# A windowed attention and MLP kernel: blocks of 48 queries instead of 56, values cast into window-ready rows, and a new opening order

## The chip, the cores and the metric

The kernel runs on one core of a Trainium2 chip. The metric is the device time of one execution in microseconds. A profiled execution gives the trace; its span runs from the first to the last instruction. Engines are named as the profile names them: PE (TensorE, with PEld for its weight loads), DVE (VectorE), ACT (ScalarE), POOL (GpSimd), SP (SyncE, which issues transfers). POOL's transfers run on the DMA queue q0, SP's on q1.

## The reference

Attention over 576 positions with a window of 32 to either side and 8 global positions (which attend to all and are attended by all), for 8 batches and 8 heads of 64; its output, seen as 4608 rows of 512, goes through an MLP whose activation is h cos h.

```python
def _attn_ref(q, k, v, global_idx):            # q, k, v: 8 x 8 x 576 x 64, fp32
    scores = np.matmul(q, k.transpose(0, 1, 3, 2)) / np.sqrt(D)
    mask = np.abs(pos[:, None] - pos[None, :]) <= 32
    mask = mask | is_global[:, None] | is_global[None, :]
    scores = np.where(mask, scores, -1e9)
    attn = np.exp(scores - np.max(scores, axis=-1, keepdims=True))
    attn = attn / (np.sum(attn, axis=-1, keepdims=True) + 1e-09)
    return np.matmul(attn, v)

def reference(...):
    x = attn_out.transpose(0, 2, 1, 3).reshape(4608, 512)
    h = x @ w_in                                # 512 x 2048
    return (h * np.cos(h)) @ w_out              # 2048 x 512
```

## The kernel before

**Tiling of attention.** Work goes by pairs of heads, 32 in all: pair `pr` is batch `pr // 4`, heads `2 (pr % 4)` and the next. A batch's 576 queries are cut into NB = 11 blocks of QB = 56 (the last block is partly padding). A block's keys are the 8 global ones and a window of W = 120, 128 in all, which fill the partitions; its queries are the 8 global ones and its own 56, C = 64 columns a head, two heads beside each other. `scores` multiplies, for four blocks at a time, keys (`kw`, the weights) by queries (`qb`), takes exp on ACT (`e`) and multiplies by `mask` on DVE (`pm`). `values` multiplies each block's `pm` (weights, 64 columns) by the block's window of values `vw` (64 values and a one, which gives the denominator) into `pv`, and normalizes into `xn`. `turn_x` transposes `xn` on PE into `xT`; for every fourth pair POOL copies the eight global queries' columns into `xT` (L483).

**Where keys, queries and values come from.** A half `s` is 4 heads, two pairs; there are 16. For the first four halves `load_qk` has POOL load keys and queries with a cast to fp16 into `kn`, `qn`, and `turned`, called by `local_k` and `local_q`, transposes them on PE; ACT and DVE copy them into `kw` and `qb`. For later halves `cast_half` has POOL write fp16 copies `k16`, `q16` to DRAM, `turn_half` has SP load them transposed into `kT`, `qT`, and DVE copies the blocks out. Values of every half are cast to `v16` in DRAM as they lie; `load_v` then has SP gather each pair's overlapping windows from it, one row of 64 values (128 bytes) per key, block and head; `load_vg` does the same for the global values. `vw`, `kw` and `qb` have four buffers. `gather` fetches the rows of the global positions; `build_globals` casts and transposes them, for 16 pairs at once. `globals_k` and `globals_q` (POOL) copy them into `kw` and `qb`.

**The MLP.** `mlp_in(t, f)` makes one of 16 groups of hidden units for 512 rows: four matmuls, a cosine on ACT, a product on DVE. `mlp_out(t, u)` adds four of 16 hidden groups to an output tile. They fill PE between the parts of attention.

**Order.** The order on each engine is the program's order, written by hand. It begins with set-up code; then the list `FRONT` names the first steps (`s2.0` is scores of pair 2, part 0; `k`, `q` local keys and queries; `g` globals; `p` values; `x` turn_x; `L` load_qk; `c` the cast of a half's values; `v` load_v and load_vg; `W` a quarter of w_in; `n` x_squares; `I` register loads). Then a loop runs steps s = 2 to 15, two pairs each, by the list `THIRD` for s = 2 and `ORDER` after that: `1` is a call of `mlp_in`, `2` one of `mlp_out`, letters `a`, `z`, `c`, `d` stand for pairs 2s to 2s + 3, and `G` calls `casts(s)`, where POOL waits for `xn` of the step (the gate, L662) and issues the casts of a later half (half 4 in step 2, half 5 in step 3, two halves in step 4, then one a step). `w_out` is loaded in one transfer at the beginning of step 2. At each step's end SP issues `turn_half(s + 2)` and the loads of values for pairs 2s + 4 and 2s + 5. After the loop the MLP work that is left runs alone.

Of the kernel before, what the change touches and what calls it, by code (L numbers as in the profile page):

```python
# [21 lines left out]
QB = 56  # L22
NB = 11
G = 8
W = 120
BP = 6
KL = 32
HY = 4
RW = 8
KPAD = 4  # L30
KP = KPAD + S // RW + 10
QP = S // RW + 6
KT = KL + S + 80
QT = S + 48
# [6 lines left out]
ORDER = "sa0 sa1 sa2 2 2 2 sz0 2 sz1 sz2 pa 1 1 2 xa pz G 1 1 2 xz n 1 1 2 kc qc 1 kd qd 2 1"  # L41

THIRD = "sa0 sa1 sa2 sz0 sz1 sz2 1 1 pa 1 1 xa pz G 1 1 kc qc xz 1 1 kd qd 1 n 1"

FRONT = ("s0.0 s0.1 s0.2 s1.0 s1.1 s1.2 k2 q2 g4 L2 p0 k3 q3 s2.0 s2.1 s2.2 g5 W0 c2 p1 x0 g6 W1 s3.0 s3.1 s3.2 g7 I "
         "p2 x1 L3 v4 v5 p3 x2 k4 q4 x3 W2 k5 q5 n0 W3 c3 v6 v7")
# [145 lines left out]
def kernel(  # L192
# [22 lines left out]
    ident16 = const.tile([P, P], FP16)  # L215
    pio2 = const.tile([P, 1], FP32)
# [7 lines left out]
    nc.sync.dma_start(gidx_col, dview(gi, 0, (0, 16), (2, G), (1, 1)))  # L224
    nc.sync.dma_start(gidx_all, dview(gi, 0, (0, P), (1, 2 * G)))
    nc.sync.dma_start(gidx_row, dview(gi, 0, (2 * G, 1), (1, 2 * G)))
# [4 lines left out]
    v16 = dram.tile([B * H * S, D], FP16)  # L231
# [4 lines left out]
    qT = [keep.tile([P, 2, QT], FP16, name=f"qT{i}") for i in range(2)]  # L236
    kn = [keep.tile([KP, 2 * 2, RW, D], FP16, name=f"kn{i}") for i in range(2)]
    qn = [keep.tile([QP, 2 * 2, RW, D], FP16, name=f"qn{i}") for i in range(2)]
    vw = [keep.tile([P, NB, 2, D + 1], FP16, name=f"vw{i}") for i in range(NV)]
    NK = 4  # L240
    kw = [keep.tile([P, NB, P], FP16, name=f"kw{i}") for i in range(NK)]
    qb = [keep.tile([P, NB, 2, C], FP16, name=f"qb{i}") for i in range(NK)]

    def cast_half(s, which):

        base = s * 4 * S * D
        for x in which:
            if x == "v":
                nc.gpsimd.dma_start(v16[s * 4 * S : (s + 1) * 4 * S].rearrange("(n r) d -> n (r d)", r=16),
                                    dview(v, base, (16 * D, 4 * S // 16), (1, 16 * D)))  # L250
            else:
                src, dst = {"k": (k, k16), "q": (q, q16)}[x]
                nc.gpsimd.dma_start(dst[s].rearrange("t (h d) -> t h d", h=4),  # L253
                                    dview(src, base, (D, S), (S * D, 4), (1, D)))

    def load_qk(s):

        base = s * 4 * S * D
        for src, dst in ((k, kn[s % 2][KPAD : KPAD + S // RW]), (q, qn[s % 2][0 : S // RW])):
            nc.gpsimd.dma_start(dst.rearrange("x h r d -> x h (r d)"),  # L260
                                dview(src, base, (RW * D, S // RW), (S * D, 4), (1, RW * D)))

    def turn_half(s):

        nc.sync.dma_start(kT[s % 2][:, :, KL : KL + S], k16[s], transpose=True)
        nc.sync.dma_start(qT[s % 2][:, :, 0:S], q16[s], transpose=True)


    qg32 = keep.tile([P, 2, 2, D], FP32)
    kg32 = keep.tile([P, 2, 2, D], FP32)  # L270
    vg32 = keep.tile([P, 2, 2, D], FP32)
# [6 lines left out]
    def index_rows():  # L278
# [5 lines left out]
        nc.vector.scalar_tensor_tensor(gidx_rows, p8, float(2 * S // G), gidx_col, ALU.mult, ALU.add)  # L284

    def gather(src, dst, half):
        rows = src.rearrange("b h s d -> (b h s) d")
        for h in range(2):
            nc.gpsimd.indirect_dma_start(
                out=dst[:, half, h], out_offset=None, in_=rows,  # L290
                in_offset=bass.IndirectOffsetOnAxis(ap=gidx_rows[:, 0:1], axis=0),
                element_offset=(half * 32 + h) * S * D)

    vg16 = keep.tile([P, 2, 2, D], FP16)

    def load_v(pr):


        b, h0 = pr // NP, 2 * (pr % NP)
        vt = vw[pr % NV]  # L300
        for h in range(2):
            lo, i0, i1 = (b * H + h0 + h) * S * D, 0, NB
            if pr == 0 and h == 0:
                nc.sync.dma_start(vt[G + 32 : P, 0, h, 0:D], dview(v16, 0, (D, W - 32), (1, D)))
                i0 = 1
            if pr % 2 and h:

                nc.sync.dma_start(vt[G : G + 104, NB - 2, h, 0:D], dview(v16, lo + 472 * D, (D, 104), (1, D)))  # L308
                nc.sync.dma_start(vt[G : G + 48, NB - 1, h, 0:D], dview(v16, lo + 528 * D, (D, 48), (1, D)))
                i1 = NB - 2  # L310
            nc.sync.dma_start(vt[G:P, i0:i1, h, 0:D],
                              dview(v16, lo + (QB * i0 - 32) * D, (D, W), (QB * D, i1 - i0), (1, D)))

    def load_vg(pr):
        for h in range(2):
            nc.sync.dma_start(
                vw[pr % NV][0:G, :, h, 0:D],
                view(vg16[(pr % 16) * G : (pr % 16 + 1) * G, pr // 16, h], (0, NB), (1, D)))


    mask = keep.tile([P, NB, 2, C], FP16)

    def build_mask():
# [24 lines left out]
        nc.vector.tensor_scalar(own, df[:, 0:1], float(W), None, ALU.is_lt)  # L348
        nc.vector.memset(own[0:G], 0.0)
        for h in range(2):  # L350
            nc.vector.tensor_tensor(
                mask[:, :, h, G:], view(nk, (1, NB), (0, QB)), view(band[:, G:], (0, NB), (1, QB)), ALU.mult)
            nc.vector.tensor_scalar(
                mask[:, :, h, 0:G], view(val, (1, NB), (0, G)), own[:, 0:1], None, ALU.mult)
# [18 lines left out]
    def build_globals(half):  # L373
        for src, dst in ((kg32, kgT), (qg32, qgT)):
            g16 = work.tile([P, P], FP16, tag="g16")
            nc.scalar.copy(g16, src[:, half].rearrange("x h d -> x (h d)"))
            t = ps.tile([P, 16 * G], FP16, tag="s", bufs=3)
            nc.tensor.transpose(t, g16, ident16)
            nc.scalar.copy(dst[:, 16 * half : 16 * half + 16], t.rearrange("x (n g) -> x n g", g=G))
        nc.scalar.copy(vg16[:, half], vg32[:, half])  # L380
# [4 lines left out]
    xT = keep.tile([P, NC, NT + 40], FP16)  # L385
# [15 lines left out]
    def turned(src, pr, n):  # L401

        t = ps.tile([P, RW, n], FP16, tag="h" if front[0] else "s", bufs=2 if front[0] else 3)
        h0 = 2 * (pr % 2)
        for r in range(RW):
            for h in range(2):
                nc.tensor.transpose(t[h * D : (h + 1) * D, r], src[:n, h0 + h, r], ident16[:n, :n])  # L407
        return t

    def local_k(pr):  # L410
        to = kw[pr % NK][:, :, G:]
        if pr < 2 * HY:
            t = turned(kn[pr // 2 % 2], pr, KP)
            nc.scalar.copy(view(to, (P, NB), (RW, W // RW), (1, RW)),  # L414
                           view(t, (QB // RW, NB), (1, W // RW), (KP, RW)))
        else:
            nc.vector.tensor_copy(to, view(kT[pr // 2 % 2][:, pr % 2], (QB, NB), (1, W)))

    def local_q(pr):
        if pr < 2 * HY:  # L420
            t = turned(qn[pr // 2 % 2], pr, QP)
        for h in range(2):
            hp = slice(h * D, (h + 1) * D)
            to = qb[pr % NK][hp, :, h, G:]
            if pr < 2 * HY:
                copy = nc.scalar.copy if h == 0 or pr < 2 else nc.vector.tensor_copy
                copy(view(to, (2 * C, NB), (RW, QB // RW), (1, RW)),
                     view(t[hp], (QB // RW, NB), (1, QB // RW), (QP, RW)))
# [3 lines left out]
    def scores(pr, g):  # L432
        kp, qp = kw[pr % NK], qb[pr % NK]
        if g == 0:
            pm_of[pr] = work.tile([P, NB, 2, C], FP16, tag="pm", name="pm")
        pm = pm_of[pr]
        g0, n = 4 * g, min(4, NB - 4 * g)
        st = ps.tile([P, 4, P], FP32, tag="s", bufs=3)
# [322 lines left out]
```

## Time and profile before

| | |
|---|---|
| runs | 396.44, 393.04, 397.9 us; median 396.44 |
| the profiled execution | 397.13 us; span 395.4 us; granted TensorE clock 0.955 |
| PE busy | 328.3 us (83%), 2678 matmuls |
| PEld busy | 174.7 us (44%) |
| DVE busy | 260.6 us (66%) |
| ACT busy | 238.8 us (60%) |
| POOL busy | 114.8 us (29%) |
| DMA packets | 188504, 47.18 MB; 177005 of them under 512 bytes |
| q1 (SP's transfers) | 124509 packets, 27.89 MB, 59.6% of 16 engines' span |
| q0 (POOL's transfers) | 63952 packets, 18.75 MB, 48.4% |

Busy shares are means over stages with different limits, and matmuls are pipelined, so a busy PE is one that has work in it. A queue's share is the time of its packets as a part of 16 engines' time; with several packets under way at once the shares can add up to more than 100%. "Us" in a row's second column is the length of a piece, and a line such as L311 is the line of the kernel that issued the instruction.

### The profile page before, as it was taken

How to read it: one execution, taken by the hardware profiler on the slowest of the kernel's cores; microseconds unless marked ns; L12 is line 12 of the kernel's file. 1: busy time of each engine (PE TensorE's matmuls, PEld its weight loads, DVE VectorE, ACT ScalarE, POOL GpSimd, SP SyncE). 2: the span in 40 equal slices, each digit the busy share in tenths (PEclk: the TensorE clock that was granted, in tenths of full speed). 3: DMA queues.
4: the chain of work that ended last, by engine and by line, in shares of the span. 5: the costliest groups of instructions: out<-in, count | busy, mean ns of one | idle time of the engine just before them, and what ended most of it. 6: DMA issues, size and time to landing. Idle time of an engine off the chain costs nothing.

```text
span 395.4 us, 7373 instructions
## 1 busy us (share of the span) xinstructions
PE 328.3 (83%) x2678; PEld 174.7 (44%) x2678; DVE 260.6 (66%) x600; ACT 238.8 (60%) x351; POOL 114.8 (29%) x250
## 2 busy tenths in 40 slices
PE   0272179576778889899999999999999979999993
PEld 0262164343434355455555555555555334444441
DVE  7744157555687768789788888888889354544300
ACT  1572066945575686677778678776777866244210
POOL 6573032504268275071443507223000100000000
PEclk9997558969999999999999999999999999999999
DMA  6989979999999999999999999999990000010121
GB/s 92 96 123 199 123 43 181 215 130 124 176 121 177 108 175 131 166 154 180 149 176 187 127 177 140 191 141 120 144 118 31 27 2 27 28 54 27 55 80 60
DMA packets 188504, 47.18 MB, mean 119 GB/s; under 512 B 177005, under 2 KB 183405, under 8 KB 188205
## 3 DMA queue, kind: packets, MB, share of 16 engines
q1 hardware_dynamic: 124509, 27.89, 59.6%
q0 software_dynamic: 63952, 18.75, 48.4%
q8 instruction: 23, 0.38, 0.5%
q14 instruction: 20, 0.16, 0.2%
HBM read 47.73 MB, written 21.23 MB: 174 GB/s over the span
## 4 chain that ended last, share of the span: by engine, by line
PE 67%; DMA 10%; DVE 8%; ACT 5%; issue 3%; SPq 3%; another core or an unknown queue 1%; POOL 0%; ACTq 0%; DVEq 0%
PE po L505 28%; PE ph L491 27%; DMA q<-in_q_dram 4%; PE st L440 4%; PE pv L452 4%; DMA vw<-vg 3%; DMA vw<-v 3%; DVE g L495 2%; PE tx L475 2%; SPq L308 2%; ACT cos L494 2%; DVE xn L463 1%; PE t L407 1%; ACT sq L524 1%
## 5 line engine op out<-in xcount | busy, mean ns | idle before, releaser
L491 PE MATMUL ph<-xT,w_in 128*128 128x512 f16 x576 | 142.8, 385 | 6.7 <-DVE g L495 5.9
L505 PE MATMUL po<-w_out,g 128*128 128x512 f16 x576 | 140.4, 380 | 5.0 <-DMA w_out<-in_moe_w_out_dram 3.6
L494 ACT ACTIVATE cos<-ph,pio 128x512 f16<-128x512 f32 x144 | 97.3, 686 | 77.2 <-PE ph L491 75.6
L495 DVE TENSOR_TENSOR g<-cos,ph 128x512 f16<-128x512 f16 x144 | 96.4, 685 | 55.0 <-ACT cos L494 52.7
L505 PEld LDWEIGHTS <-g 128*128 128x128 f16 x576 | 55.4, 98 | 67.7 <-issue 5.2
L491 PEld LDWEIGHTS <-w_in 128*128 128x128 f16 x576 | 54.1, 99 | 69.4 <-issue 13.1
L442 ACT ACTIVATE e<-st 128x512 f16<-128x512 f32 (+1 forms) x96 | 47.6, 561 | 14.3 <-PE st L440 9.3
L443 DVE TENSOR_TENSOR pm<-e,mask 128x512 f16<-128x512 f16 (+1 forms) x96 | 37.0, 405 | 23.8 <-ACT e L442 21.9
L662 POOL COPY gate<-xn 1x1 f16<-1x1 f16 x14 | 2.5, 182 | 143.3 <-DVE xn L463 143.3
L452 PE MATMUL pv<-vw,pm 128*64 128x65 f16 x704 | 20.6, 204 | 23.1 <-issue 10.3
L440 PE MATMUL st<-qb,kw 128*128 128x128 f16 x352 | 30.8, 238 | 4.2 <-ACT e L442 1.5
L440 PEld LDWEIGHTS <-kw 128*128 128x128 f16 x352 | 26.3, 108 | 14.2 <-POOL xT L483 2.9
L463 DVE TENSOR_TENSOR xn<-pv,r_all 128x768 f16<-128x768 f32 x32 | 30.6, 958 | 1.9
L452 PEld LDWEIGHTS <-pm 128*64 128x64 f16 x704 | 16.6, 117 | 27.3 <-issue 19.0
L253 POOL DMA_DIRECT2D q<-in_q_dram x12 | 27.6, 2304 | 0.0
L414 ACT COPY kw<-t 128x1320 f16<-128x1320 f16 x8 | 10.1, 1257 | 28.7 <-PE t L407 28.7
L483 POOL COPY xT<-xg 128x4 f16 x64 | 20.5, 320 | 22.0 <-DVE xT L478 18.6
L510 ACT COPY o<-po 128x512 f32<-128x512 f32 x18 | 10.5, 586 | 22.4 <-PE po L505 21.9
L524 ACT ACTIVATE sq<-xn 128x1536 f16<-128x1536 f16 x16 | 23.6, 1474 | 0.0
L430 DVE COPY qb<-qT 64x616 f16<-64x616 f16 x48 | 22.1, 460 | 0.3
L253 POOL DMA_DIRECT2D k<-in_k_dram x12 | 21.2, 1765 | 0.3 <-issue 0.3
L512 DVE COPY o<-po 128x512 f32<-128x512 f32 x18 | 12.3, 685 | 12.1 <-PE po L505 12.0
(106 smaller groups left out, 269.2 us busy)
## 6 DMA issues: line engine op xcount, KB each, us to landing
out_dram<-o SPq DMA_DIRECT2D x36, 256.0 KB
vw<-v SPq DMA_DIRECT2D x47, 165.0 KB
v<-in_v_dram POOLq DMA_DIRECT2D x16, 288.0 KB
k<-in_k_dram POOLq DMA_DIRECT2D x12, 288.0 KB
q<-in_q_dram POOLq DMA_DIRECT2D x12, 288.0 KB
vw<-v SPq DMA_DIRECT2D x16, 135.0 KB
w_in<-in_moe_w_in_dram POOLq DMA_DIRECT2D x4, 512.0 KB
w_out<-in_moe_w_out_dram POOLq DMA_DIRECT2D x1, 2048.0 KB
```

What stands on the lines that cost most here:

```text
L253: nc.gpsimd.dma_start(dst[s].rearrange("t (h d) -> t h d", h=4), dview(src, base, (D, S), (S * D, 4), (1, D)))
L430: nc.vector.tensor_copy(to, view(qT[pr // 2 % 2][hp, pr % 2], (QB, NB), (1, QB)))
L440: nc.tensor.matmul(st[:, j], kp[:, g0 + j], view(qp[:, g0 + j], (1, P)), start=True, stop=True)
L442: nc.scalar.activation(e[:, :n], st[:, :n], AF.Exp, scale=scale)
L443: nc.vector.tensor_tensor(view(pm[:, g0], (1, n * P)), view(e, (1, n * P)), view(mask[:, g0], (1, n * P)), ALU.mult)
L452: nc.tensor.matmul(pv[r0 : r0 + C, j // 6, c0 : c0 + 65], pm[:, j, h], vp[:, j, h], start=True, stop=True)
L463: nc.vector.tensor_tensor(view(xn, (384, 2), (D, 6), (1, D)), view(pv, (512, 2), (65, 6), (1, D)), view(rp, (6, 2), (1, 6), (0, D)), ALU.mult)
L491: nc.tensor.matmul(ph, w_in16[:, j, f * P : (f + 1) * P], xT[:, j, t * TT : (t + 1) * TT], start=(j == 0), stop=(j == NC - 1))
L494: nc.scalar.activation(cos, ph, AF.Sin, bias=pio2)
L495: nc.vector.tensor_tensor(g16[:, f], cos, ph, ALU.mult)
L505: nc.tensor.matmul(po, g16[:, f, s * P : (s + 1) * P], w_out16[:, f], start=(f == 0), stop=(f == NF - 1))
L524: nc.scalar.activation(sq, view(xn, (1, 2 * BP * P)), AF.Square, accum_out=x_sq[:, s : s + 1])
```

## The change

**Blocks.** QB becomes 48 and NB 12, which divides 576 without padding; W becomes 112, so a block has KW = 120 keys and 2 x C = 112 query columns. Scores are three groups of four equal blocks (before: four, four and three). Keys are taken circularly: the window of block 0 begins with the last 32 keys and that of the last block ends with the first ones, and the mask takes them out. `kn` and `qn` have no padding and are not zeroed; `local_k` makes two copies on ACT and a small one on POOL for a turned pair, and wraps 32 columns of `kT` on DVE for each later half.

**Values.** `v16` becomes four buffers, used in turn by the halves, each with 48 rows (the place in the block) of 4 heads x 12 blocks x (64 values and a one). They are first filled with ones by SP. The cast writes 64-value runs into them, leaving the ones. `load_v` is four transfers a pair, whose runs hold all blocks of one or two heads. `vw` is ordered by head, then block. The global values lie repeated for every block in `vgw` (`spread_globals`), and `load_vg` copies whole rows.

**Globals.** `gather` handles 8 pairs at a time, in three transfers instead of six, four times in all: at the beginning, and in steps 2, 6 and 10 at `G`, ahead of the casts. The steps `b` and `t` (`copy_globals`; `turn_globals` and `spread_globals`) in those same steps cast, transpose and spread them.

**Opening.** New set-up order, `FRONT`, and `w_out` in four transfers (`O`) at the end of `FRONT`. The set-up fills `qb` with zeros on ACT.

```diff
-QB = 56
-NB = 11
-W = 120
+QB = 48
+NB = 12
+W = 112
+KW = G + W
+GP = 8
-THIRD = "sa0 sa1 sa2 sz0 sz1 sz2 1 1 pa 1 1 xa pz G 1 1 kc qc xz 1 1 kd qd 1 n 1"
-FRONT = ("s0.0 s0.1 s0.2 s1.0 s1.1 s1.2 k2 q2 g4 L2 p0 k3 q3 s2.0 s2.1 s2.2 g5 W0 c2 p1 x0 g6 W1 s3.0 s3.1 s3.2 g7 I "
-         "p2 x1 L3 v4 v5 p3 x2 k4 q4 x3 W2 k5 q5 n0 W3 c3 v6 v7")
+ORDER = "sa0 sa1 sa2 2 2 2 sz0 2 sz1 sz2 pa 1 1 2 xa pz G 1 1 2 xz n 1 1 2 kc qc 1 b kd qd 2 t 1"
+THIRD = "sa0 sa1 sa2 sz0 sz1 sz2 1 1 pa 1 1 xa pz G 1 1 kc qc xz 1 1 b kd qd 1 n t 1"
+FRONT = ("g0 s0.0 s0.1 s0.2 c1 k1 q1 g1 B s1.0 s1.1 s1.2 v2 v3 g2 g3 W0 L2 c2 k2 q2 p0 s2.0 x0 s2.1 s2.2 W1 I "
+         "k3 q3 p1 s3.0 x1 s3.1 s3.2 L3 c3 g4 g5 k4 q4 p2 v4 v5 W2 x2 p3 W3 k5 q5 x3 n0 v6 v7 g6 g7 O0 O1 O2 O3")
...
-    v16 = dram.tile([B * H * S, D], FP16)
+    VB = 4
+    VH = NB * (D + 1)
+    v16 = [dram.tile([QB, 4 * VH], FP16, name=f"v16_{i}") for i in range(VB)]
...
-                nc.gpsimd.dma_start(v16[s * 4 * S : (s + 1) * 4 * S].rearrange("(n r) d -> n (r d)", r=16),
-                                    dview(v, base, (16 * D, 4 * S // 16), (1, 16 * D)))
+                nc.gpsimd.dma_start(dview(v16[s % VB], 0, (D + 1, 4 * NB), (4 * VH, QB), (1, D)),
+                                    dview(v, base, (QB * D, 4 * NB), (D, QB), (1, D)))
...
     def load_v(pr):
+        vt, src, base = vw[pr % NV], v16[pr // 2 % VB], 2 * (pr % 2) * VH
+        row = 4 * VH
+        p0 = G + KL
+        nc.sync.dma_start(view(vt[p0 : p0 + QB], (1, 2 * VH)), dview(src, base, (row, QB), (1, 2 * VH)))
+        nc.sync.dma_start(view(vt[p0 + QB : KW], (1, 2 * VH)),
+                          dview(src, base + D + 1, (row, W - KL - QB), (1, 2 * VH)))
+        base += (QB - KL) * row
+        nc.sync.dma_start(vt[G:p0, :, 1:].rearrange("x h n d -> x h (n d)"),
+                          dview(src, base, (row, KL), (VH, 2), (1, VH - D - 1)))
+        nc.sync.dma_start(vt[G:p0, :, 0], dview(src, base + VH - D - 1, (row, KL), (VH, 2), (1, D + 1)))
     def load_vg(pr):
         for h in range(2):
+            p0 = (pr % GP * 2 + h) * G
+            nc.sync.dma_start(vw[pr % NV][0:G, h], vgw[p0 : p0 + G])
...
     def scores(pr, g):
+        st = ps.tile([KW, 4, 2 * C], FP32, tag="s", bufs=3)
+        for j in range(4):
+            nc.tensor.matmul(st[:, j], kp[:, 4 * g + j], view(qp[:, 4 * g + j], (1, 2 * C)), start=True, stop=True)
...
+        nc.sync.dma_start(gidx_col, dview(gi, 0, (0, 2 * GP), (2, G), (1, 1)))
+        nc.sync.dma_start(gidx_all, dview(gi, 0, (0, P), (1, 2 * G)))
         nc.gpsimd.iota(p_i, pattern=[[0, 1]], base=0, channel_multiplier=1)
         load_qk(0)
+        nc.vector.memset(zero16, 0.0)
+        nc.vector.memset(vgw, 1.0)
+        for t in v16:
+            nc.sync.dma_start(t.rearrange("r (n x) -> r n x", n=4), view(vgw[0:QB], (0, 4), (1, VH)))
+        for i in range(NK):
+            nc.vector.memset(kw[i][:, NB - 1, KW - KL :], 0.0)
+            nc.scalar.copy(view(qb[i], (1, NB * 2 * C)), view(zero16, (0, NB * 2 * C)))
...
+        gather(k, kg32, 0)
+        gather(q, qg32, 0)
+        cast_half(0, "v")
+        gather(v, vg32, 0)
+        load_qk(1)
+        copy_globals("k")
+        local_k(0)
+        copy_globals("q")
+        turn_globals("kq", 0)
+        build_mask()
+        local_q(0)
+        load_v(0)
+        load_v(1)
...
     def casts(s):
+            if s % 4 == 2 and s // 4 < 3:
+                for src, dst in ((k, kg32), (q, qg32), (v, vg32)):
+                    gather(src, dst, s // 4 + 1)
             for n in range(4, 2 * B):
                 if s == (n - 2 if n < 7 else n - 3):
                     cast_half(n, "vkq")
-            if s == 4:
-                for src, dst in ((k, kg32), (q, qg32), (v, vg32)):
-                    gather(src, dst, 1)
```

## The prediction

> **What bounds the kernel now.** I read the profiled execution (span 395.4 us, time 397.13) in this order: the 40 slices, the stretches between the first score matmuls of successive steps, the chain of waits, the DMA queues by window, the timeline of one steady step. A "step" s is two pairs of heads (2s, 2s+1). Two of the slice rows:
>
> ```profile
> PE   0272179576778889899999999999999979999993
> PEclk9997558969999999999999999999999999999999
> DMA  6989979999999999999999999999990000010121
> ```
>
> PE is thinly used for a quarter of the span, full from slice 16, and the DMA engines are busy from the start to slice 30. The stretches (columns: length, then busy time and count of PE, PEld, DVE, ACT, POOL, then clock, DMA share, GB/s) are: up to the first scores, step 0 and 1, steps 2, 3, 4, then a steady step:
>
> ```profile
> 0.00:20.86 20.86, 3.61 (x67) 2.90 (x68) 14.83 (x47) 7.79 (x13) 12.54 (x24) 1.00 0.91 105
> 20.86:55.47 34.61, 16.92 (x285) 14.53 (x284) 14.70 (x39) 12.33 (x19) 10.88 (x28) 0.71 1.09 130
> 55.47:74.98 19.51, 16.81 (x185) 9.26 (x184) 14.20 (x36) 15.57 (x25) 10.81 (x24) 0.82 0.98 154
> 74.98:99.68 24.70, 15.19 (x119) 7.91 (x118) 13.05 (x30) 14.22 (x21) 5.30 (x10) 0.86 1.55 145
> 99.68:118.22 18.54, 14.45 (x126) 7.33 (x127) 13.63 (x32) 11.67 (x19) 7.64 (x16) 1.00 1.41 145
> 192.29:209.20 16.91, 16.91 (x143) 9.07 (x142) 14.58 (x34) 12.92 (x19) 5.55 (x12) 1.00 1.57 167
> ```
>
> In the steady step PE is busy 16.91 of 16.91 us: there only PE's own work counts. Before 99.68 no engine fills its stretch. The chain of waits says what does:
>
> ```profile
> 34.52 5.40 SPq L308
> 39.97 0.36 SPq L309
> 40.38 9.38 DMA vw<-v
> ...
> 70.87 17.34 DMA q<-in_q_dram
> ```
>
> 15 us go to issuing and landing the window loads of values (vw) for pairs 2 and 3, and 17 us to the q cast of half 4, the first whose keys and queries come by transposing loads; step 4 cannot start before them. The queues in 46:57, 57:79 and 79:88 (packets, MB, share of 16 engines; q1 carries SP's transfers, q0 POOL's):
>
> ```profile
> q1 hardware_dynamic: 5744, 0.72, 97.3%
> ```
>
> ```profile
> q0 software_dynamic: 3180, 3.74, 103.2%
> ```
>
> ```profile
> q0 software_dynamic: 4644, 0.59, 100.4%
> q1 hardware_dynamic: 4685, 0.61, 87.5%
> ```
>
> First: 0.973 x 11 us x 16 / 5744 = 30 ns for each 128-byte row of vw, nothing else moving; q0 stood empty for 11 us because POOL waited 15.5 us for the xT copy (L478) before issuing w_in, v and w_out. Second: weights; without some 45 engine-us for the two v casts, 318 engine-us over 3148 packets, 0.10 us each. Third: the k and q casts of half 4, 4608 runs, 9 us, 31 ns a run. A second such pair of casts ran in 6 us (99:105, share 152.7%), so one cast costs 3 to 4.5 us of q0.
>
> **The change, part by part.**
>
> *Window loads.* Now a pair needs 2 x 1320 rows of 128 bytes and 2 x 88 for the globals: 2816 x 30 ns / 16 = 5.3 us of q1. Afterwards 48 + 32 rows of 3120 bytes, 64 of 1430, 64 of 130, and 16 of 1560 for the globals. The nearest row is the output stores, 2048 bytes each: in 330:395, 11.9% x 65 us x 16 / 1643 = 75 ns, so 115 ns for 3120 bytes (estimate by size). Sum: 80 x 115 + 80 x 55 + 64 x 30 = 15.5 engine-us, 1.0 us of q1 a pair. Issues on SP go from 2 (even pairs) or 4 (odd) to 4, beside the same two for globals, at 0.3 to 0.4 us where nothing holds them (L309, L311); long ones (5.77 us at L308) came while q1 was full, and I let them go with the rows.
>
> *v casts.* Now a half is 16 long packets, some 1.4 us of q0 (22 engine-us). Afterwards it is 48 x 48 = 2304 runs of 128 bytes, written 130 bytes apart. Nearest row: the k and q casts, also 2304 runs, written in aligned places: 3 to 4.5 us. I take 3.7, so +2.3 us of q0 a half. Whether odd places cost more no row shows; bounds below nothing: 1.4 us (no worse than now), above: 9 us (each run written as two). POOL's issue goes from 0.5 us to the 1.1 us between the starts of successive k and q issues; in steady state POOL idles 11 us a step at the gate (L662, 143.3 us over 13), which hides it. The steady q0 load a half goes from 9 + 1.4 to 9 + 3.7 = 12.7 of 16.9 us: hidden; without that cover it is paid in full.
>
> *PE in a step.* Scores: 22 matmuls of 128 columns become 24 of 112; values 44 become 48 of 65. The timeline of a steady step:
>
> ```profile
> 196.58 0.55 PE L440 MATMUL st<-qb,kw 128*128 128x128 f16 x7
> 197.06 0.57 PE L452 MATMUL pv<-vw,pm 128*64 128x65 f16 x22
> 197.56 0.39 PE L491 MATMUL ph<-xT,w_in 128*128 128x512 f16 x1
> ```
>
> 22 value matmuls take 0.50 us, 23 ns each, so +4 is +0.09 us. Four scores take 0.22 us (195.49 to 195.71), 55 ns each for 128 columns; at 112, 49 ns: 24 x 49 against 22 x 55, -0.03. Turning x (12 transposes) and the 64 MLP matmuls stay. Together +0.06 us a step, +1 over 13 steps.
>
> A weight load is now 120 wide instead of 128 (L440). Loads of 64 columns show 117 ns (L452) beside 98 for 128 (L505), so odd widths do load slower, but the values' 23 ns pitch shows such loads overlapping the matmuls. I take zero. If a load of 108 ns (L440) set the pitch, a step would pay 24 x 108 - 22 x 55 = 1.4 us. The Trainium skill ("TensorE: Matmul & The Clock Gate", section on Fast Weight Load) says the quick load is only taken with exactly 128 weights; its LDWEIGHTS section gives columns / 1.2 ns, 53 ns for 64 columns. The trace's 23 ns pitch contradicts the second; by that formula 120 columns would be 100 ns and the step +1.2 us.
>
> *Other engines.* Exp on 448 instead of 512 and 384 columns: between 596 and 493 ns, 545; the mask product between 428 and 358, 393. A pair saves 0.05 us of ACT and 0.03 of DVE; the extra key wrap on DVE costs some 0.1 us. PE's full step covers all three.
>
> *Until the first scores (20.86 us).* The four memsets that held load_qk(0) back (1.18 us wait) go; six gathers become three (1 us of POOL each); ACT now makes one pair, not two, and the globals (before: 18.39 to 20.2) follow pair 0's keys at once. New: four zero fills of qb on ACT (1.25 us each, as the kw copy; 5 us, hidden until keys land near 8.5) and four fills of v16 (1.2 MB on SP, some 3 us of DMA beside load_qk(0); the v cast waits for them on POOL, with gather v, load_qk(1) queued behind). Keys 9, ACT about 4 us of small copies, POOL's globals: first scores at 14 (13 to 18).
>
> *First steps.* ACT in the new list: 12 x 0.545 + 5 key copies of 1.4 + 5 query copies of 0.65 + spreading the value globals 0.9 + squares 1.7 = 19.5 us, and 3 to 6 us of draining between pairs: step 2 starts near 38 (34 to 45). POOL issues W2, W3, L3 and c3 ahead of the last xT copies, so q0's 11 empty us shrink.
>
> *Half 4.* Now q0 decides. Four qk loads, 576 packets x 0.1 / 16 = 3.6 each: 14.4; w_in and w_out, 2048 packets each: 26; v casts 0 to 3, 4 x 3.7 = 15; from 4 us on, without a gap, 59. The second batch of gathers sits here, in step 2, ahead of the casts: landed near 61 (2 us receipt, from load_qk(0)'s last packets to its user), and ACT's copy_globals at "b", due near 51, waits for it: a new stall of 10 us with step 2's last MLP work and all of step 3 behind it. Then three casts, 11 us, 2 to land, 3 to transpose: keys for pair 8 at about 76, 5 to 6 later with POOL's remaining waits: 82. Step 4 starts at 83 instead of 99.68: -17 (a gapless queue and 3 us casts: 72, -28; the full 11 us gap and 4.5 us casts: 95, -5).
>
> *Steps 4 to 7* take 75.7 us now; their MLP groups (12, 16, 16, 16 of 0.86 us) and attention (3.1 us) give 64. Lost now: late keys in step 4, gathers behind two halves of casts in step 4 (POOL waits 7.1 us for vg), late vw (6.67 us in the chain, at 159.85). With vw at a fifth I take -6 (0 to -11).
>
> Sum: -17 - 6 + 1 = -22; 397.1 - 22 = 375, against a median of 396.4.
>
> **Rivals.** (1) *Odd-placed runs make q0 the bound* (slower). Let a v cast cost c. Half 15 then lands at about 61 + 5c + 11(9 + c) + 3 = 163 + 16c and is needed in step 14, now at 275. At c = 7 (48 ns a run) all gain is gone, at 7.5 it is 2% slower, at 9 it is 163 + 144 = 307, +32: 428. For: a write off its alignment, many runs sharing a line. Against: aligned runs take 3 to 4.5, and q1 gives up 8.6 us a step. The Trainium skill ("DMA: Bandwidth & Descriptors", Specifications) says transfers under 512 bytes are read, modified and written; it speaks for the loads and against the cast, and has no price. (2) *Half 4 comes no earlier*: gathers behind w_out, POOL's waits and the longer casts fill the time that vw gave up; only steps 4 to 7 gain little: 392. For: q0 carries 59 us before it. (3) *Unhidden 120-wide loads*: 1.4 us x 13 = +18 on the forecast: 393. By the skill's formula, 16. (4) *The loads do not get cheaper*, being spread over 32 or 48 partitions: 394; against it, 75 ns for 2 KB.
>
> **How the numbers follow.** Forecast 0.57 (358 to 388), (1) 0.2 counting milder forms above 404, (2) 0.11, (3) 0.07, (4) 0.05. A measurement of this kernel tells about 2% from no change: below 388.5 faster, 0.59 (a little of the others), within 0.21, above 404.4 slower, 0.2. The forecast's own bounds are 397 - 39 = 358 and 397 - 3 = 394; taking in the others, and finer luck in steps 0 to 3, 354 to 405.
>
> **What would show it.** Right: first scores near 14, step 2 near 38, step 4 near 83, vw gone from the chain, q1's packets down by some 80,000 and q0's up by 37,000, steady steps at 17.0. Wrong: v casts over 5 us on q0, steps of 18 us with PE waiting for kT or qT, score matmuls 100 ns apart, step 4 after 95.

## The result

| | runs | median us (lowest to highest) |
|---|---|---|
| before, beside it | 4 | 396.94 (393.04 to 397.9) |
| after | 4 | 441.24 (440.36 to 441.31) |

The ratio is 1.113, with a 95% interval of 1.105 to 1.121: the change makes the kernel 11% slower, where 375 us had been forecast. The profiled execution of after has a span of 438.7 us. From its page: the slices, the two queues (packets, MB, share of 16 engines) and two DMA issues (count, KB each, median us from issue to landing):

```profile
PE   0145478178869499299999699987999988999994
PEclk9999999669989979789999699999899999999998
DMA  5999999999999999999999969999961000110021
...
q0 software_dynamic: 100608, 18.75, 113.6%
q1 hardware_dynamic: 44450, 29.72, 34.6%
...
v<-in_v_dram POOLq DMA_DIRECT2D x16, 288.0 KB, 12.7
...
q<-in_q_dram POOLq DMA_DIRECT2D x12, 288.0 KB, 18.4
```

q1 lost 80,059 packets and q0 gained 36,656, as forecast. But q0's packets now take 113.6% of the engines' span (48.4% before; over 100% is possible because several packets are under way at once), and PE has slices of 1 to 6 tenths up to the middle of the span and past it, where before stayed at 9. The stretches, cut as in the prediction (length, busy time and count of PE, PEld, DVE, ACT, POOL, then clock, DMA share, GB/s): up to the first scores, steps 0 and 1, steps 2, 3, 4, then step 8 and step 14, the first with no casts:

```profile
0.00:24.20 24.20, 1.89 (x34) 1.47 (x35) 8.67 (x37) 9.46 (x15) 9.54 (x21) 1.00 1.48 108
24.20:57.82 33.62, 17.33 (x328) 15.68 (x328) 15.15 (x38) 15.90 (x28) 14.01 (x31) 1.00 1.49 152
57.82:89.10 31.28, 18.80 (x192) 10.23 (x191) 14.75 (x35) 16.38 (x28) 15.58 (x30) 0.87 2.22 164
89.10:108.82 19.72, 15.08 (x125) 8.39 (x124) 13.07 (x31) 14.94 (x25) 7.12 (x14) 0.86 1.19 96
108.82:128.40 19.58, 14.54 (x132) 7.53 (x133) 14.66 (x33) 12.78 (x19) 9.40 (x17) 1.00 2.34 111
202.01:219.67 17.66, 17.17 (x150) 9.19 (x149) 15.26 (x35) 13.31 (x20) 8.67 (x18) 1.00 2.42 131
320.07:337.05 16.98, 16.98 (x150) 9.28 (x148) 14.26 (x36) 12.86 (x19) 0.18 (x1) 1.00 0.49 121
```

The last line shows what a step costs when no cast runs: 16.98 us with PE never idle, the predicted 17.0. Everything before it is longer. The chain of waits (start, length, what) says why:

```profile
2.22 8.17 DMA v<-vgw
10.68 12.72 DMA v<-in_v_dram
...
43.98 21.57 DMA v<-in_v_dram
...
220.00 6.23 SPq L265
226.32 5.28 SPq L266
...
234.78 11.39 DMA vw<-vgw
...
274.05 11.35 DMA vw<-v
...
294.46 11.58 DMA vw<-vgw
```

v casts stand on it (12.7 and 21.6 us from issue to landing, the second behind other loads on q0), the issue of the transposing loads behind the casts (L265, L266), and window loads of 11 us each, though few rows are left in them. The starts of steps (first score matmul), with the two experiments that matter most beside them:

| us | before | after | rows of 160 bytes | the last version |
|---|---|---|---|---|
| first scores | 20.86 | 24.20 | 19.16 | 19.05 |
| step 2 | 55.47 | 57.82 | 47.82 | 47.71 |
| step 3 | 74.98 | 89.10 | 73.95 | 68.79 |
| step 4 | 99.68 | 108.82 | 93.63 | 88.58 |
| step 8 | 175.37 | 202.01 | 169.52 | 162.51 |
| step 14 | 276.87 | 320.07 | 274.81 | 265.64 |

After loses 9 us to before by step 4, 17.5 in steps 4 to 7 (93.2 against 75.7) and 16.6 in steps 8 to 13 (118.1 against 101.5): 43 in all, the difference of the two spans (438.7 and 395.4).

### The profile page after: what moved, and what is told of

It is laid out like the page before. It is cut to its first block, busy times and chain, and to the rows that moved or that the text cites. A ratio compares the mean times of both kernels' runs of the same rounds, so it can differ in the third digit from the quotient of the medians.

```text
span 438.7 us, 7702 instructions
## 1 busy us (share of the span) xinstructions
PE 341.2 (78%) x2778; PEld 182.2 (42%) x2778; DVE 263.9 (60%) x599; ACT 247.1 (56%) x379; POOL 131.0 (30%) x261
## 3 DMA queue, kind: packets, MB, share of 16 engines
q0 software_dynamic: 100608, 18.75, 113.6%
q1 hardware_dynamic: 44450, 29.72, 34.6%
## 4 chain that ended last, share of the span: by engine, by line
PE 42%; DMA 25%; issue 9%; SPq 8%; ACT 6%; POOL 5%; DVE 2%; POOLq 1%; ACTq 0%; DVEq 0%
PE po L514 19%; PE ph L500 17%; DMA v<-in_v_dram 8%; DMA vw<-v 7%; DMA vw<-vgw 5%; DMA qg<-in_q_dram,gidx_rows 3%; PE pv L461 2%; SPq L266 2%; PE st L450 2%; SPq L265 2%; DMA v<-vgw 2%; ACT cos L503 2%; DVE g L504 1%; PE tx L484 1%; POOL v L249 1%
## 5 line engine op out<-in xcount | busy, mean ns | idle before, releaser
L514 PE MATMUL po<-w_out,g 128*128 128x512 f16 x576 | 144.9, 389 | 1.0 <-DVE o L521 0.9
L504 DVE TENSOR_TENSOR g<-cos,ph 128x512 f16<-128x512 f16 x144 | 97.2, 686 | 67.2 <-ACT cos L503 64.4
L452 ACT ACTIVATE e<-st 120x448 f16<-120x448 f32 x96 | 46.3, 544 | 43.8 <-PE st L450 43.0
L450 PE MATMUL st<-qb,kw 128*120 128x112 f16 x384 | 35.0, 245 | 35.3 <-ACT e L452 10.8
L453 DVE TENSOR_TENSOR pm<-e,mask 120x448 f16<-120x448 f16 x96 | 37.3, 395 | 26.5 <-ACT e L452 23.7
L450 PEld LDWEIGHTS <-kw 128*120 128x120 f16 x384 | 33.1, 159 | 46.3 <-issue 31.4
L461 PE MATMUL pv<-vw,pm 120*56 120x65 f16 x768 | 21.6, 209 | 14.4 <-DMA vw<-vgw 14.2
L461 PEld LDWEIGHTS <-pm 120*56 120x56 f16 x768 | 17.6, 118 | 18.4 <-issue 13.8
L492 POOL COPY xT<-xg 128x4 f16 x64 | 21.6, 338 | 8.6 <-DVE xT L487 5.2
L484 PE MATMUL tx<-ident,xn 128*128 128x128 f16 x192 | 17.3, 231 | 7.5 <-DVE xn L472 6.7
L249 POOL DMA_DIRECT2D v<-in_v_dram x16 | 20.3, 1272 | 9.1 <-issue 4.0
L437 DVE COPY qb<-t 64x576 f16<-64x576 f16 x8 | 6.1, 760 | 24.3 <-ACT qb L437 24.3
## 6 DMA issues: line engine op xcount, KB each, us to landing
v<-in_v_dram POOLq DMA_DIRECT2D x16, 288.0 KB, 12.7
q<-in_q_dram POOLq DMA_DIRECT2D x12, 288.0 KB, 18.4
```

The lines of the kernel that those rows point to most:

```text
L249: nc.gpsimd.dma_start(dview(v16[s % VB], 0, (D + 1, 4 * NB), (4 * VH, QB), (1, D)), dview(v, base, (QB * D, 4 * NB), (D, QB), (1, D)))
L450: nc.tensor.matmul(st[:, j], kp[:, 4 * g + j], view(qp[:, 4 * g + j], (1, 2 * C)), start=True, stop=True)
L452: nc.scalar.activation(e, st, AF.Exp, scale=scale)
L453: nc.vector.tensor_tensor(view(pm[:, 4 * g], (1, n)), view(e, (1, n)), view(mask[:, 4 * g], (1, n)), ALU.mult)
L461: nc.tensor.matmul(pv[r0 : r0 + C, j // 6, c0 : c0 + 65], pm[:, j, h], vp[0:KW, h, j], start=True, stop=True)
L504: nc.vector.tensor_tensor(g16[:, f], cos, ph, ALU.mult)
```

## Experiments: where a run of 128 bytes is written

The suspect is the v cast, 2304 runs of 128 bytes written 130 bytes apart. Six kernels change that place or its surroundings, and a seventh takes the values by their old path.

**Rows of 96 and of 80 elements** (192 and 160 bytes for 64 values and a one; in the first also a work tile is shared to make room). The loads and everything else stay.

```diff
-    VH = NB * (D + 1)
+    PT = 96        # and 80
+    VH = NB * PT
-   dview(v16[s % VB], 0, (D + 1, 4 * NB), (4 * VH, QB), (1, D))
+   dview(v16[s % VB], 0, (PT, 4 * NB), (4 * VH, QB), (1, D))
```

> As the changed kernel, but a block's row of values is 96 wide (64 values, a one, 31 unused ones) instead of 65, so that each 128-byte run of the v cast begins on a multiple of 64 bytes and shares no 64-byte line with its neighbour; the window loads carry half as many bytes again. Theory A (the runs are slow because they lie at odd places and share lines): a v cast falls from 8 us to 3 to 4.5 us of q0, q0's share from 114% to some 75%, mean of its 128-byte packets from 71-94 ns to 32-40, total 375 to 395. Theory B (they are slow because each engine steps through 48 rows 6 KB apart): no faster cast, total 435 to 450, a little slower for the longer loads. Theory C (the new blocks and first steps cost the time, the cast only fills what is left): q0 falls, the total stays over 425.

> As pitch96 with rows 80 wide: runs begin on multiples of 32 bytes, every second one off a 64-byte line. Theory A with lines of 32 bytes: as fast as pitch96. Theory A with lines of 64 bytes: some runs still share lines, total between pitch96 and the changed kernel, 400 to 435. Theory B: 435 to 445. Theory C: over 425.

Measured: 398.34 us at 192 bytes, ratio 1.003 [0.999, 1.006]; 394.18 us at 160, ratio 0.994 [0.990, 0.998]. Their pages, 192 first:

```profile
q0 software_dynamic: 100608, 18.75, 58.4%
...
v<-in_v_dram POOLq DMA_DIRECT2D x16, 288.0 KB, 6.4
```

```profile
q0 software_dynamic: 100608, 18.75, 60.0%
...
v<-in_v_dram POOLq DMA_DIRECT2D x16, 288.0 KB, 6.5
...
q<-in_q_dram POOLq DMA_DIRECT2D x12, 288.0 KB, 9.3
```

The same number of packets on q0 takes half the time, and a v cast lands in 6.5 instead of 12.7 us. The whole loss of 44 us goes with the 130-byte pitch. What is left is 0.6% better than before. Theory B is out, since both kernels still step through far rows, and so is theory C. Lines of 64 bytes are out too, since every second run of the 160-byte rows starts off one. Theory A's 375 to 395 us missed the 192-byte rows by 3 us.

**The runs in another order** (rows of 130 bytes; neighbouring runs follow each other in the cast).

```diff
-   dview(v16[s % VB], 0, (D + 1, 4 * NB), (4 * VH, QB), (1, D)), dview(v, base, (QB * D, 4 * NB), (D, QB), (1, D))
+   dview(v16[s % VB], 0, (4 * VH, QB), (D + 1, 4 * NB), (1, D)), dview(v, base, (D, QB), (QB * D, 4 * NB), (1, D))
```

> The changed kernel with the two outer loops of the v cast exchanged: the same runs at the same odd places, but in order of rows, so that an engine writes neighbouring runs one after another and, up to the ends of its rows, no other engine writes into its lines. Theory A (odd places themselves): still 57 ns a run, total 435 to 445. Theory A' (lines shared between engines that write at the same time): 32 to 40 ns a run, total 380 to 400. Theory B (steps over far rows): also faster, 380 to 400; pitch96 tells B from A'.

Measured: 480.47 us, ratio 1.216 [1.208, 1.225]. The order did not help; it made the kernel slower again, past everything that the theories had given (445 at most). The cast now also reads its values in another order (each run 12 KB behind the one before), so this run doesn't tell the order of the writes from that of the reads, and no other tells why:

```profile
q0 software_dynamic: 100608, 18.75, 132.5%
```

**The old value path in the new kernel** (a row of 64 for every key, cast in long packets, windows loaded in 128-byte rows, no fills).

```diff
-    v16 = [dram.tile([QB, 4 * VH], FP16, name=f"v16_{i}") for i in range(VB)]
+    v16 = dram.tile([B * H * S, D], FP16)
...
+            nc.sync.dma_start(vt[G:KW, h, i0:i1, 0:D],
+                              dview(v16, lo + (QB * i0 - KL) * D, (D, W), (QB * D, i1 - i0), (1, D)))
```

> The changed kernel with the old path of values alone: v16 as the values lie, written in long runs, and windows loaded in rows of 128 bytes (112 keys x 12 blocks x 2 heads a pair); blocks of 48, globals and first steps as changed, v16 is not filled. Theories A and B: without the scattered cast what is left of the change is near the kernel before or better: q0's share near 50%, q1's near 60%, total 385 to 405. Theory C: 425 or more.

Measured: 393.9 us, ratio 0.995 [0.991, 0.998]. So the blocks of 48 and the new opening are not what costs 44 us; nor do they gain more than some half a per cent by themselves. Beside the 394.18 us of the 160-byte rows it also says that the window-ready rows, cheaply written, gained nothing over the old path of values.

**Misplaced, but with no neighbour near** (rows of 192 bytes, values from the second element on).

```diff
-   dview(v16[s % VB], 0, (PT, 4 * NB), (4 * VH, QB), (1, D))
+   dview(v16[s % VB], 1, (PT, 4 * NB), (4 * VH, QB), (1, D))
```

> Rows of 96 elements (192 bytes) as in the run of that pitch, but the 64 values of a row start at its second element, so that every run of 128 bytes is written at a place 2 bytes past an aligned one while no two runs touch the same 64 bytes. Theory M (a run that starts and ends inside a 64-byte piece is written slowly, alone): v casts of some 8 us as with 130-byte rows, q0 over 100%, 430 to 440 us. Theory S (two neighbouring runs that touch the same 64-byte piece hold each other up): casts of 3 to 5 us, q0 near 58%, 398 us within 2%. Between the two if both play.

Measured: 437.43 us, ratio 1.096 [1.087, 1.104].

```profile
q0 software_dynamic: 100608, 18.75, 102.1%
...
v<-in_v_dram POOLq DMA_DIRECT2D x16, 288.0 KB, 11.2
```

The time and q0's share are theory M's, and S is not needed: two bytes off are enough, although no two runs come near each other.

**Rows of 72 and of 66 elements** (144 and 132 bytes; `PT = 72`, `PT = 66`).

> Rows of 72 elements (144 bytes): every run starts at a multiple of 16 bytes, runs of neighbouring blocks touch the same 64-byte piece in three places of four and never overlap in 16 bytes. Theory S with pieces of 64 bytes: slow casts, some 6 to 8 us each, 425 to 440 us. Theory S with pieces of 32 bytes or less: half of the boundaries or none are shared, casts of 4 to 5 us, 394 to 410 us. Theory M: as slow as 130-byte rows wherever the start is no multiple of 64 bytes (three of four), 420 to 440 us.

> Rows of 66 elements (132 bytes): every run of 128 bytes starts at a multiple of 4 bytes, one in eight of them at a multiple of 32. Theory M2 (only a start that is no multiple of 4 bytes is slow): casts of 3 to 5 us, q0 near 60%, 394 to 400 us. Theory M32 (what counts is where in a piece of 32 or 64 bytes the run starts and ends, and 144-byte rows were on the way, with q0 at 75% against 60% for 160): casts of 6 to 9 us, q0 at 90 to 120%, 425 to 445 us.

Measured: 397.38 us at 144 bytes, ratio 0.995 [0.991, 1.000]; 417.24 at 132, ratio 1.051 [1.042, 1.060]. For 144, S with pieces of 32 bytes had given 394 to 410 and all else 420 or more, so M with pieces of 64 bytes is out. At 132 the time lies between the two ranges (M2 at most 400, M32 at least 425), while q0's share is M32's. The packets at 144 are slower on average than at 160 (43 against 33 ns), but not enough to matter; at 132 they are (144 first):

```profile
q0 software_dynamic: 100608, 18.75, 75.2%
...
v<-in_v_dram POOLq DMA_DIRECT2D x16, 288.0 KB, 8.8
```

```profile
q0 software_dynamic: 100608, 18.75, 103.5%
...
v<-in_v_dram POOLq DMA_DIRECT2D x16, 288.0 KB, 11.2
```

Put in order by the share of runs that start at a multiple of 32 bytes, with the mean time of q0's 128-byte packets from the traces (k, q and v casts together; the runs of k and q are in aligned places in every kernel):

| kernel | v runs that start on 32 | mean packet | q0 | ratio |
|---|---|---|---|---|
| 192 or 160 bytes | all | 33 ns | 58%, 60% | 1.003, 0.994 |
| 144 bytes | 1 in 2 | 43 ns | 75% | 0.995 |
| 132 bytes | 1 in 8 | 66 ns | 104% | 1.051 |
| 192 bytes, 2 off | none | 69 ns | 102% | 1.096 |
| 130 bytes (after) | 1 in 16 | 77 ns | 114% | 1.113 |

M2, a rule of 4 bytes, is out: at 132 bytes every run keeps it. M32 fits the order of the rows but for the last two, where the closer rows of after take 77 against 69 ns; crowding may add that, and no run separates it. Nor does the time follow q0's share alone: 132 bytes and 192 with 2 off have nearly the same share and differ by 4 points in the ratio.

The means hide how the time is spent. The median packet takes 32 ns in every row. What differs is how many take over 100 ns: under 1% at 192 and 160 bytes, 5.5% at 144, and 16% in the last three rows, where these slow ones take 226, 249 and 306 ns on average. One v cast of after shows it (that of half 7, in 137.2:138 and in 138.5:141, where nothing else moves):

```profile
q0 software_dynamic: 967, 0.12, 240.4%
```

```profile
q0 software_dynamic: 853, 0.11, 550.8%
```

By share x length x 16 / packets a run takes 32 ns in the first window and 258 in the second. So an odd run is not slow at once: somewhat over half of a cast's 2304 runs go at full pace, and then the stream stalls. Why it starts fast is not shown. At 144 bytes all runs start on 16, and fewer are off; whether a place halfway is cheaper, or too few odd runs came to stall the stream, is not told apart either.

The Trainium skill ("DMA: Bandwidth & Descriptors", section "How a descriptor splits into AXI transactions") tells of beats of 32 bytes, for reads; that writes go by the same pieces is an inference from this table. Its rule that transfers under 512 bytes are read, modified and written (Specifications) does not tell these rows apart, since all of them are runs of 128 bytes.

## Experiments: where the rest of the forecast went

With rows of 160 bytes the v casts and the window loads are cheap, and still step 4 starts at 93.6, not 83, and the end gains some 2 us (ratio 0.994), not 22. From here on all kernels have these rows. The chain of waits of that kernel in its first steps, and the first link of the kernel with the old value path, which has no fills:

```profile
2.22 8.12 DMA v<-vgw
...
12.13 6.56 DMA vg<-in_v_dram,gidx_rows
...
62.34 7.91 DMA kg<-in_k_dram,gidx_rows
```

```profile
4.40 6.31 DMA kg<-in_k_dram,gidx_rows
```

Fills of v16, which POOL's v cast waits for; the gather of v, queued behind that cast; and in step 2 the second batch of gathers. Without fills the gather of k had landed at 10.7 us and the first scores came at 15.12.

**Three fills behind the first window load, the gather of v ahead of the cast; then the second gathers early as well** (at the end of `FRONT`).

```diff
+        for t in v16[1:]:                       # behind local_q(0), on SP
+            nc.sync.dma_start(...)
-        cast_half(0, "v")
         gather(v, vg32, 0)
+        cast_half(0, "v")
# second kernel also:
-FRONT = "... g6 g7 O0 O1 O2 O3"
+FRONT = "... g6 g7 R1 O0 O1 O2 O3"              # R1: the gathers of step 2
```

> Rows of 80 elements, and the order of the opening changed: the gather of v stands ahead of the first v cast on q0, and three of the four fills of the value scratch are issued after the first queries are laid out, ahead of the first window load. Theory O (the opening's gain was lost to the fills on SP and to a gather that waits behind the cast): first scores at 15 to 16 us instead of 19.2, step 1 at 25 instead of 29.0; step 2 then waits for the second batch of gathers and takes back most of it (step 4 at 92 to 93 instead of 93.6), so 392 to 394 us. Rival (the start is set by the casts of k and q and their transposes): first scores stay within 1 us of 19.2. If each step hands its lead on: 390 us.

> The same, and the second batch of gathers is issued at the end of the opening's list, ahead of the output weights' loads, instead of in step 2 behind its gate. Theory O with step 2 bound by the gathers: step 2 falls from 26 us to 18 to 20, step 4 starts at 86 to 89 instead of 93.6, end at 386 to 389 us. Rival H (step 4 waits for half 4, cast and turned at its own pace): step 2 gets shorter, step 3 longer by the same, step 4 within 2 us of 93.6, end at 392 to 395 us.

Measured: 397.46 us, ratio 0.999 [0.995, 1.003], first scores at 18.42, step 4 at 97.2; with early gathers 394.84, ratio 0.993 [0.990, 0.997], step 4 at 94.4. The first part tells nothing of theory O: SP had nothing to wait for and issued all four fills at once, while the v cast now stood behind the gather. Step 1 starts at 32.91 instead of 29.01: there the chain runs through that cast (9.0 us to land) and the window loads behind it (6.1 and 5.5 us). The second gains 2.6 us beside the first: step 2 takes 22.5 instead of 25.4 us, and step 3 grows by 1.0, not by the same. So theory O's 386 to 389 was missed; the end and step 4 are rival H's, its reason only in part.

**Three fills from ACT's queue, behind `local_q(0)`.**

```diff
+        for t in v16[1:]:
+            nc.scalar.dma_start(...)
```

> Rows of 80 elements; of the four fills of the value scratch only the first is issued at the start, the other three from ACT's queue after the first queries are laid out (in the run before, all four still went at once, since SP had nothing else to wait for). The order of casts and gathers is the one of the change. Theory O (the fills hold the first loads, gathers and the first v cast): the cast goes out at 6 to 8 us instead of 10.6, the gather of k lands at 11 to 12 instead of 15, first scores at 15 to 17 instead of 19.2; by step 4 part of it is left: 92 to 93, end 391 to 394 us. Rival (one fill delays as much as four, since the first transfers start at 5 us anyway): scores at 18.5 to 19.5, 394 us.

Measured: 396.84 us, ratio 0.998 [0.994, 1.003]. The gather of k lands at 12.2 (14.0 with four fills at the start) and the first scores start at 16.86, as theory O said. But the v cast still goes out at 10.6 us, not at 6 to 8: the one fill that it needs lands no sooner without the other three behind it. Then the chain goes on with the fills, and POOL's wait for them (us in total, times, longest) is longer:

```profile
4.41 7.77 DMA kg<-in_k_dram,gidx_rows
...
16.45 8.98 DMA v<-vgw
```

```profile
POOL v L250 <- DMA v<-vgw: 11.0, 2, 7.2
```

Cast 1 now waits 7.2 us, step 1 starts at 31.65 instead of 29.01, and step 4 at 96.8. The fills on the chain need 8 to 9 us from issue to landing in both places. That three fills at the start hold up the gather of k, by 1.8 us, is shown; the lead is lost again, and the 391 to 394 us of theory O was missed.

**The v cast behind the next keys' copies in every step, and all three together.** In steps with casts the 160-byte kernel takes 17.5 to 18.0 us. Its timeline in step 9 (start, length, what):

```profile
201.25 2.18 POOL L254 DMA_DIRECT2D q<-in_q_dram  x1
...
202.24 1.19 DVE L427 COPY kT<-kT 128x64 f16<-128x64 f16 x1
```

POOL's issue of the q cast ends at 203.43, and the small wrap copy of keys, begun at 202.24, ends at the same moment. Eight of this kernel's twelve copies begin during such an issue, and each of them ends within 0.02 us of it (1.04 to 1.48 us); the other four take 0.17 to 0.25. Not all of DVE is held: a product begun at 201.64, in the same issue, took its usual 0.69 us. In the kernel with the old value path the v cast's issue is 0.5 instead of 1.2 us, q's issue ends sooner, and the copy comes after it. The copy's line in both kernels (minimum, median and maximum ns), 160 bytes first:

```profile
L427 DVE COPY kT<-kT x12: 173/1114/1483, 91.3 to 289.9; 128x64 f16<-128x64 f16 x12
```

```profile
L426 DVE COPY kT<-kT x12: 173/176/489, 96.5 to 288.4; 128x64 f16<-128x64 f16 x12
```

```diff
-ORDER = "... xa pz G 1 1 2 xz n 1 1 2 kc qc 1 b kd qd 2 t 1"      # G: gathers, casts of v, k, q
+ORDER = "... xa pz G 1 1 2 xz n 1 1 2 kc qc 1 b kd qd V 2 t 1"    # G: gathers, casts of k, q; V: of v
```

> Rows of 80 elements; in each step the v cast is issued after the copies of the next keys and queries instead of ahead of the k and q casts. Theory D (the v cast's issue, 1.2 us instead of 0.5, pushes the q cast's issue onto the wrap copy of keys on DVE, which then takes 1.1 to 1.5 us instead of 0.17 and holds the scores up): wrap copies of 0.2 us, steps 8 to 13 at 17.0 to 17.2 us instead of 17.6, end at 389 to 392 us. Rival (the steps with casts are longer because the casts' traffic delays loads): steps stay at 17.5 to 18.0, 394 us. If the v cast now lands too late for its loads: over 396 us.

> The three together: rows of 80 elements, three fills later from ACT's queue, the second batch of gathers at the end of the opening's list, the v cast after the copies. If the parts add: opening -3 us at step 4, gathers -3, steps 4 to 13 -0.5 us each: 382 to 386 us. If step 4 waits for half 4 whatever came before, only the later steps gain: 388 to 392 us.

Measured: 394.57 us, ratio 0.994 [0.989, 0.998], and 392.58, ratio 0.990 [0.984, 0.995]. The steps split: 8, 9, 11 and 12 fall to 16.99 to 17.04 us, as theory D said, but step 10, which gathers, rises from 17.52 to 19.20, and step 7 from 18.00 to 18.64. So part of the gain was given back in other steps, and the time is the rival's 394. All three together end just above the 388 to 392 of only the later steps gaining; the parts did not add.

**The v cast late only where nothing is gathered** (from step 7 on), with the early gathers; and the same with three fills from ACT's queue, ahead of the copy of the global keys.

```diff
+                    casts(s, "kq" if s > 6 and s % 4 != 2 else "vkq")
+                elif step == "V":
+                    if s > 6 and s % 4 != 2:
+                        casts(s, "v")
```

> Rows of 80 elements, the second batch of gathers at the end of the opening's list, and the v cast after the copies of the next keys and queries only in the steps from 7 on that gather nothing; elsewhere it stays ahead of the k and q casts. Theory D (the collision of the wrap copy with the q cast's issue makes the steps 17.5 to 18.0 instead of 17.0): steps 7 to 9, 11 and 12 at 17.0 to 17.1, step 10 (gathers) back at 17.5, so -3 us against the early gathers alone is too much to ask but -2.5 is expected; the early gathers -2: 389 to 390.5 us. Rival (a step saved is given back in the gather steps): 392 to 394 us.

> The same, and three of the four fills issued from ACT's queue ahead of the copy of the global keys, at about 7 us. Theory O: the gather of k lands at 12 to 13 instead of 15 and the first scores come at 16.5 to 17.5 instead of 19.2, while cast 1 no longer waits as it did with the fills at 16 us; 2 us of it are left at step 4: 387 to 389 us. Rival (whatever is saved ahead of step 2 is waited for in steps 2 and 3): within 1 us of the run beside it.

Measured: 385.82 us, ratio 0.979 [0.975, 0.982], and 388.15 for the other, ratio 0.983 [0.980, 0.986] (before beside them: 394.65). The first beats both kernels of this case, and is faster than either theory had given. Its stretches, up to step 2, step 2, steps 4 to 7, steps 8 to 13, and then the last three of the kernel with 160-byte rows:

```profile
0.00:47.71 47.71, 19.04 (x362) 16.99 (x363) 23.99 (x75) 25.36 (x43) 23.52 (x52) 1.00 1.19 179
47.71:68.79 21.08, 17.53 (x192) 9.86 (x191) 14.25 (x35) 15.70 (x28) 15.60 (x30) 1.00 1.06 196
88.58:162.51 73.93, 67.97 (x578) 35.60 (x579) 62.10 (x135) 51.17 (x81) 37.58 (x65) 0.98 1.53 167
162.51:265.64 103.13, 102.59 (x891) 55.49 (x890) 89.70 (x205) 78.94 (x121) 44.88 (x91) 1.00 1.37 172
```

```profile
47.82:73.95 26.13, 18.29 (x192) 10.01 (x191) 14.86 (x35) 16.48 (x28) 15.58 (x30) 0.91 1.41 208
93.63:169.52 75.89, 68.10 (x579) 35.88 (x579) 63.24 (x135) 51.42 (x82) 37.49 (x62) 0.98 1.47 164
169.52:274.81 105.29, 103.19 (x890) 55.26 (x891) 91.72 (x205) 78.79 (x121) 45.78 (x94) 1.00 1.29 165
```

Step 2 is 5.1 us shorter (gathers off its path), steps 4 to 7 2.0 (no run says why), steps 8 to 13 2.2 (the collision; 2.5 was expected): 9.2 us by step 14 in these two executions; by the ratios to before, 0.994 and 0.979, some 6 us. In the second kernel the fills did not go at 7 us: ACT's queue had nothing to wait for, and issued the three between 2.1 and 5.3 us. The v cast then waited until 12.9 us, the gather of k landed at 15.1, later than with all fills on SP, and the kernel is 2 us slower than the first. Its time lies in the 387 to 389 that was expected, but by chance, and fills at 7 us remain untried.

## Why the prediction was wrong, step by step

**The failed step is the cost of a v cast.** The term was 3.7 us of q0 a half, with bounds of 1.4 and 9. In after, the three casts of half 5, from their first packet to their last, take 12.9 us; with 160-byte rows 7.4, with 2.5 for the v cast; so the v cast in after costs some 8 us (12.9 - 7.4 + 2.5), part of which may fall on the k cast behind it. The bounds held it and the choice did not: the nearest row was a run of the same length in another place, and the place was the whole difference (ratio 1.113 at 130 bytes, 0.994 at 160). Rival (1) named this mechanism and its price from 7 us on.

**Rival (1) was priced too low.** By its 163 + 16c, 8 us put the data for step 14 at 291, 16 us late; step 14 started 43 us late. Its sum took q0 as always busy and the other queue as untouched. But POOL still waits at its gate for the step's last value product, so that the casts start late in each step (waits of POOL in 202:320, us in total, times, longest):

```profile
POOL gate L673 <- DVE xn L472: 56.1, 5, 14.7
```

And while a slow cast runs, SP's transfers wait too: the window loads took 11 us each in the chain, though their packets are few. Their packets of 3120 bytes took 475 ns at the median in those half microseconds in which 20 or more of q0's runs took over 100 ns, and 136 where none did. The cast of q, queued behind those of v and k, lands 18.4 us after its issue instead of 9.3.

**Until the first scores**, 14 was forecast, 24.2 measured, 19.16 with the cast healed. "Some 3 us of DMA" for the four fills was the mis-sized term: the first takes 8 us to land, which holds the v cast until 10.6, and the gather of v behind it. The gather of k lands at 14.0 against 10.7 in the kernel without fills. The bounds, 13 to 18, missed it.

**Step 4** was forecast at 83 (72 to 95) and came at 108.8. With the healed cast it is 93.6, inside, but near the end that was given for a full gap in q0 and casts of 4.5 us; in the last version 88.6. The wait for gathers in step 2 was foreseen at 10 us; with the healed cast 7.9 stand in the chain.

**Steps 4 to 7** were to shrink from 75.7 to 70, and took 93.2. With the healed cast they take 75.9; with the old value path 72.0; in the last version 73.9. The loads did become cheap, but POOL got a longer issue in their place (1.2 instead of 0.5 us a v cast). What else keeps them from 70 stays open.

**The wrap of keys** was priced at 0.1 us of DVE and PE's full step was named as its cover. Alone it takes 0.17; beside the q cast's issue 1.1 to 1.5, just ahead of the scores, and the cover failed: PE is busy 103.19 of 105.29 us in steps 8 to 13. Theory D is shown by the steps of 17.0 us once the v cast's issue is moved. The Trainium skill ("SBUF — State Buffer", section "SBUF: two separate sides") says that DVE copies in a two-port mode and GpSimd share a pair of ports under an exclusive lock; the copy that ends with POOL's issue agrees, though the trace does not show the lock itself.

**Right** were: packets moved from q1 to q0; a step without casts at 16.97 to 16.98 us, and with it 24 scores of 112 columns, 48 value products, and 120-wide weight loads at no cost, which puts rival (3) out (each takes 135 ns at the median, all of it hidden); the loads' cheapness, which puts rival (4) out (q1 34.6% instead of 59.6%). The signs named for wrong, v casts over 5 us and step 4 after 95, are what came.

## What to carry to other kernels

Price a scattered DMA write by where its pieces start and end, not by their length alone: padding 65 fp16 values to a row of 80 took 47 us off this kernel, and q0's share told it at a glance. When a transfer is moved to another queue, follow also its issue on the engine and what runs on the neighbour just behind it. A fill at the start is not free: whoever waits for it gets all of its latency. And an instruction late in the program's order goes early if its queue has nothing to wait for.

## What the runs showed of the hardware

- Runs of 128 bytes written to DRAM by casting DMAs took 33 ns on average where all started at multiples of 32 bytes. Where those of v did not, the mean over k, q and v casts was 43 ns (half of the v runs off), 66 to 77 (most or all off) and 100 (all but 1 in 16 off, and in another order). The median stayed at 32: in a cast at 130 bytes over half of the runs went at full pace, and then they took some 260 ns each.
- A copy of 64 columns on DVE that began during POOL's issue of a strided cast ended with it, eight times of eight in the kernel with rows of 160 bytes: 173 ns became 1037 to 1483.
- A fill of 360 KB issued at 2.2 us, with three more behind it, landed 8.1 us later, and one issued at 16.5 us took 9.0, with q0 busy beside them both times.
